# RetNet into gMLP on one core: k transposed in head pairs by 128x128 matmuls, q from the seventh block on by DMA

## The chip, the cores and the metric

One core of one Trainium2 chip. The metric is device time in microseconds; the kernel before took 252.29 us, the median of 3 runs (251.16 to 252.97).

## The reference

Retention over 8 batches, 8 heads, 576 positions, head size 64; its output, all heads side by side (512 wide), is the input of a gated MLP block that mixes along the sequence:

```python
scores = q @ k.T / sqrt(64)
ret = (scores * gamma[h] ** (i - j) * (i >= j)) @ v     # B,H,S,64
x = ret.transpose(0, 2, 1, 3).reshape(B, S, 512)
u, v = split(gelu(x @ w_in), 2)                         # 512 -> 2 x 512
v_n = (v - mean(v)) / sqrt(var(v) + 1e-6) * g_ln
v_s = w_sg @ v_n + b_sg                                 # w_sg: 576 x 576, over positions
out = x + (u * v_s) @ w_out
```

q, k, v, the weights and the output are float32; the kernel's matmuls are bfloat16.

## The kernel before

The 8 x 576 rows are cut into 18 blocks (j) of 256 rows, each of two chunks (c) of 128. The decay goes into q and v as a factor by row (the casts), so a block needs only scores, a causal mask and a state carried from chunk to chunk. A chunk's 128 rows lie on 64 partitions as (p, a), two rows side by side; c picks the half of the partitions. Stages of a block, with their lines:

- `load` (L93): k, q and v from DRAM, three transfers of 512 KB on SP's queue (more where a block crosses a batch). The pool `ld` holds three blocks.
- `cast` (L231, L238, L241): to bfloat16 with the decay factor, on POOL from block 1 on.
- `T` (L260): k and q transposed on PE, 64 matmuls of 64x64 (half of the partitions by one head), into two PSUM tiles x0 and x1, one for each chunk. ACT copies chunk 0's (L263), DVE chunk 1's (L264), each with k and q together.
- `Sc` (L279): scores, half of the heads at a time; DVE multiplies with the mask (L284, `ret`).
- `Z` (L308): the state, k times v, in PSUM (`zp`); ACT copies it (L319, `zb`).
- `inter` and `intra` (L346): the output `ot` in PSUM tag z, from the state and q, then from `ret` and v. ACT copies it to `xT` (L367), with the heads on partitions and columns as w_in's rows are.
- `V` (L374): x times the v half of w_in, into PSUM tag z; ACT takes the gelu (L377, `vg`). `moments`, `power`, `center`, `norm` make the normalized v (DVE, POOL, ACT).
- `U` (L432): the u half, into x0 and x1; ACT's gelu makes `uT`.
- `W` (L445): the mix along the sequence, a finished batch's 8 pieces spread over later blocks by `mix`; DVE multiplies with u (L449, `gT`).
- `O` (L457, L460): w_out, and x added by four matmuls with the identity, into x0 and x1; ACT copies (L462), SP stores 512 KB.

Heads: `hd(r, kk)` is 4r + kk, where r is the half of the partitions on which a head's transposed k and q lie and kk its column. A head's output goes to half h % 2, column h // 2 of `ot`, so that 128-row chunk c of w_in is its rows 128c to 128c + 127.

The order is written by hand (`manual_schedule`): each engine and each DMA queue runs in the order of the code, and waits by semaphores where data or buffers aren't ready. SP's transfers use eight semaphores in turn, so each also waits for the one eight before it. The head (L503 to L577) does blocks 0 to 2, casts the weights, and builds the transposed w_sg. In `load_head` SP's queue has block 0, the v half of w_in (`load_w("v")`), block 1, the u half, block 2; ACT's queue has the bias rows and 32 partitions of block 2. DVE casts the v half (L509) before V(0), POOL the u half (L519) before U(0). The loop (j from 3) does in turn: load j+3; half of the scores of j+1; intra(j); O; W; V(j); W; T(j+2); state matmuls and the other half of the scores of j+1; W; U(j).

Of the kernel before, what the change touches and what calls it, by code (L numbers as in the profile page):

```python
# [12 lines left out]
BF = mybir.dt.bfloat16  # L13
# [20 lines left out]
def kernel(  # L34
# [12 lines left out]
    nc = tc.nc  # L47
# [3 lines left out]
    KK = H // 2  # L51
    NT = 2 * S // 128
    NCH = B * S // 128
    NB = NCH // 2
# [19 lines left out]
    def ps2(name, shape, tag, dt=F32):  # L74
        return psD.tile(shape, dt, name=name, tag=tag)

    loaded = {}

    def load(j, eng=None, piece=None):
# [7 lines left out]
        for dst, src in ((qk[:, 1], k), (qk[:, 0], q), (vf, v)):  # L87
# [29 lines left out]

    def load_w(part):
        src = {"v": moe_w_in[:, F2:], "u": moe_w_in[:, :F2], "sg": moe_w_sg[:128 * KK], "out": moe_w_out}[part]
        nc.sync.dma_start(stage[part], src.rearrange("(c p) f -> p c f", p=128))  # L120
        if part == "sg":
            nc.sync.dma_start(wst5[:], moe_w_sg[128 * KK:])

# [93 lines left out]
    blk = {}  # L217
# [25 lines left out]
    def half(x):  # L243
        return slice(64 * x, 64 * x + 64)

    def hd(r, kk):
        return KK * r + kk

    def T(j):
        s = blk[j]  # L250
        tp = [ps2("tp", [128, 2, 2, KK, 64], f"x{c}", BF) for c in range(2)]
        rows = [[], []]
        for n, part in enumerate("kq"):
            for a in range(2):
                for kk in range(KK):
                    for c in range(2):
                        for r in range(2):
                            rows[c].append((r, 64, lambda o=tp[c][half(r), n, a, kk, :],
                                            i=s[part + "b"][half(c), a, hd(r, kk), :], c=c:
                                            nc.tensor.transpose(o, i, ident[half(c), half(c)])))  # L260
        interleave(rows)
        s["T"] = [w2.tile([128, 2, 2, KK, 64], BF, name=f"qkT{c}") for c in range(2)]
        nc.scalar.copy(s["T"][0][:], tp[0][:])  # L263
        nc.vector.tensor_copy(s["T"][1][:], tp[1][:])  # L264

    def Sc(j, g, tag="y"):
        s = blk[j]
        qkT = s["T"]
        if g == 0:
            s["ret"] = w2.tile([128, 2, KK, 2, 128], BF, name="ret")  # L270
        sc = ps2("sc", [128, 2, 2, 2, 128], tag)
        rows = [[], []]
        for x in range(2):
            kk = 2 * g + x
            for a in range(2):
                for r in range(2):
                    for c in range(2):
                        rows[r].append((c, 128, lambda o=sc[half(c), r, x, a, :], kk=kk, a=a, r=r, c=c:
                                        nc.tensor.matmul(o, qkT[c][half(r), 0, a, kk, :], qkT[c][half(r), 1, :, kk, :],  # L279
                                                         start=True, stop=True, skip_group_check=True)))  # L280
# [3 lines left out]
        nc.vector.tensor_tensor(  # L284
            s["ret"][:, :, 2 * g:2 * g + 2].rearrange("p r x a t -> p r x (a t)"),
            sc[:].rearrange("p r x a t -> p r x (a t)"),
            msk[:].rearrange("p a t -> p (a t)").unsqueeze(1).unsqueeze(1).to_broadcast([128, 2, 2, 256]),
            op=Alu.mult)
# [35 lines left out]
    def states(j, cross):  # L324


        s = blk[j]
        if "ot" not in s:
            s["ot"], s["begun"] = ps2("ot", [128, 2, KK, 2, 64], "z"), set()
        rows = [[], []]  # L330
        for r in range(2):
            c = 1 - r if cross else r
            m = (2 * j + c) % NT
            if m == 0:
                continue
            n = 32 if m == MID else 64
            for kk in range(KK):
                ro, ko = hd(r, kk) % 2, hd(r, kk) // 2
                rows[r].append((ro, 2 * n, lambda c=c, r=r, kk=kk, ro=ro, ko=ko, n=n:
                                attend(j, c, ro, s["ot"][half(ro), c, ko, :, :n], zbs[2 * j + c][half(r), kk, :],  # L340
                                       s["T"][c][half(r), 1, :, kk, :n])))
        return rows

    def attend(j, c, ro, o, *args):
        begun = blk[j]["begun"]
        nc.tensor.matmul(o, *args, start=((c, ro) not in begun), stop=True, skip_group_check=True)  # L346
        begun.add((c, ro))
# [4 lines left out]
    def intra(j):  # L352
        s = blk[j]
        rows = [[], []]
        for kk in (2, 3, 0, 1):
            for a in range(2):
                for r in range(2):
                    h = hd(r, kk)
                    ro, ko = h % 2, h // 2
                    for c in range(2):  # L360
                        rows[c].append((ro, 128, lambda c=c, a=a, r=r, kk=kk, h=h, ro=ro, ko=ko:
                                        attend(j, c, ro, s["ot"][half(ro), c, ko], s["vb"][half(c), a, h, :],
                                               s["ret"][half(c), r, kk, a, :])))
# [3 lines left out]
        nc.scalar.copy(xT[:, c0:c0 + 2].rearrange("p c k (t a) -> p (c k) a t", a=2),  # L367
                       ot[:].rearrange("p c k a t -> p (c k) a t"))
# [82 lines left out]
    def O(j):  # L451
        c0 = (2 * j) % (2 * RING)
        ob = w2.tile([128, 2, DM], F32, name="ob", tag="ob")
        for t in range(2):
            op = ps2("op", [128, DM], f"x{t}")
            for c in range(KK):
                nc.tensor.matmul(op[:], gTs[0][:, c, 128 * (c0 + t):128 * (c0 + t) + 128], w_out[:, c, :],  # L457
                                 start=(c == 0), stop=False, skip_group_check=True)
            for kk in range(KK):
                nc.tensor.matmul(op[:, 128 * kk:128 * kk + 128], xT[:, c0 + t, kk, :], ident[:],  # L460
                                 start=False, stop=True, skip_group_check=True)
            nc.scalar.copy(ob[:, t], op[:])  # L462
        nc.sync.dma_start(outf[256 * j:256 * j + 256, :].rearrange("(t p) d -> p t d", t=2), ob[:])
# [24 lines left out]
                os.append((2 * KK * (b + 1), odone[0]))  # L488
                odone[0] += 1

    HEAD = 3
    V_IN, U_IN = slice(F2, 2 * F2), slice(0, F2)

    def scores(j):
# [9 lines left out]
    fill_spares()  # L504
    cast(0, "q", nc.vector)
    cast(0, "v", nc.gpsimd)
    T(0)
    scores(0)
    nc.vector.tensor_copy(w_in[:, :, V_IN], stage["v"])  # L509
    load_w("sg")  # L510
# [3 lines left out]
    V(0)  # L514
    build_g()
    cast(1, "v", nc.gpsimd)
    T(1)
    scores(1)
    nc.gpsimd.tensor_copy(w_in[:, :, U_IN], stage["u"])  # L519
    load_w("out")  # L520
# [11 lines left out]
    split3(0, S)  # L532
    norm(0)
    load(4)
    T(2)
    moments(1, 0)
    scores(2)
    moments(1, 1)
# [17 lines left out]
    for n in range(2 * SB):  # L556
        build_wT(n)
    norm(2)
    T(3)
    Sc(3, 0)  # L560
    Z(3, 0)
    release(2)
# [2 lines left out]
    cast(4, "q", nc.gpsimd)  # L565
    cast(4, "v", nc.gpsimd)
    mix()
    T(4)
    Z(3, 1)
    inter(3)  # L570
    Sc(3, 1)
# [6 lines left out]

    for j in range(HEAD, NB):
        nx, nn = j + 1 < NB, j + 2 < NB  # L580
        if j > HEAD and j + 3 < NB:
            load(j + 3)
        if nx:
            Sc(j + 1, 0)
            Z(j + 1, 0)
        intra(j)
        if j > HEAD:
            moments(j - 1, 1)
            power(j - 1)
# [62 lines left out]
```

## Time and profile before

| what | value |
|---|---|
| runs | 251.16, 252.97, 252.29 us; median 252.29 |
| profiled execution | 254.49 us |
| its span (first to last instruction) | 252.7 us |
| mean granted TensorE clock | 0.952 |
| PE busy | 209.3 us (83%) |
| DVE, ACT, POOL busy | 159.7, 143.9, 112.1 us |
| moved by DMA | 42.82 MB, mean 169 GB/s |

How to read the rows that follow. A row of the timeline is start, duration (us), engine, line, operation, output<-input, shapes, count, and in brackets how long the engine was idle before it and what released it. The chain of work that ended last is followed back from the end, and its rows are start, duration, engine and line; "issue" there is time in which the engine waited for nothing that the profile shows. In the slices (40 equal parts of the span) a digit is the busy share in tenths. A row of windows has, for each engine, busy time and instructions, then the granted clock, the mean busy share of the 16 DMA engines, and GB/s. Queue rows give packets, MB and the share of 16 engines' time; rows of DMA issues give count, KB each and us from issue to landing. PE is the matmuls, PEld their weight loads.

### The profile page before, as it was taken

To read this page: it belongs to the slowest core of one execution; us is meant where nothing else is said; L and a number is where in the kernel's file an instruction comes from. 1 tells how busy PE (TensorE), PEld (TensorE's weight loads), DVE (VectorE), ACT (ScalarE), POOL (GpSimd) and SP (SyncE) were. 2 spreads that over 40 slices of the span, in tenths; PEclk is the share of its full clock that TensorE was granted. 3 is DMA by queue.
4 is the path that set the end of the run, shared out by engine and by line. 5 is a ranking of instruction groups with operands and counts; after the bars stand their busy time and mean duration, and the time that the engine had idled before them with its cause. 6 is when DMAs were issued, how large, how long until landed. Compare 5 with 4: busy or idle time off the path is not lost.

```text
span 252.7 us, 9232 instructions
## 1 busy us (share of the span) xinstructions
PE 209.3 (83%) x4142; PEld 145.1 (57%) x4163; DVE 159.7 (63%) x274; ACT 143.9 (57%) x211; POOL 112.1 (44%) x88
## 2 busy tenths in 40 slices
PE   0466667776799899879999979979999999999992
PEld 0433445455566666746677655647677675666551
DVE  7683987495647768857686682557595766745300
ACT  3524253675257786585675655667766758554152
POOL 6325741679923583580835638062828101101000
PEclk9998587995899999999999997999999999999999
DMA  6999999999900979980659890969382012021234
GB/s 185 313 291 247 273 308 214 206 258 182 244 6 4 289 203 281 249 153 5 195 141 237 175 258 6 237 134 284 122 230 88 21 67 86 3 83 58 110 138 194
DMA packets 63592, 42.82 MB, mean 169 GB/s; under 512 B 1529, under 2 KB 56825, under 8 KB 63554
## 3 DMA queue, kind: packets, MB, share of 16 engines
q1 hardware_dynamic: 62720, 41.83, 66.0%
q8 instruction: 32, 0.52, 1.0%
q10 hardware_dynamic: 834, 0.41, 0.8%
q14 instruction: 6, 0.05, 0.1%
HBM read 32.80 MB, written 9.44 MB: 167 GB/s over the span
## 4 chain that ended last, share of the span: by engine, by line
PE 75%; ACT 9%; DVE 8%; issue 5%; DMA 2%; ACTq 0%
PE wp L445 16%; PE hu L432 13%; PE op L457 13%; PE hv L374 12%; PE ot L346 6%; PE sc L279 5%; PE tp L260 4%; PE op L460 3%; DVE ret L284 3%; PE zp L308 3%; ACT qkT L263 2%; DMA rows<-in_moe_g_ln_dram 2%; ACT vg L377 2%; ACT xT L367 1%; DVE gT L449 1%
## 5 line engine op out<-in xcount | busy, mean ns | idle before, releaser
L395 POOL TENSOR_TENSOR rs<-rs,mhalf 128x2 f32<-128x2 f32 x18 | 19.0, 1058 | 101.9 <-DVE rs L390 78.9
L449 DVE TENSOR_TENSOR gT<-wp,uT 128x288 bf16<-128x288 f32 (+1 forms) x48 | 26.6, 555 | 44.1 <-PE wp L445 44.1
L284 DVE TENSOR_TENSOR ret<-sc,mask 128x1024 bf16<-128x1024 f32 x36 | 44.0, 1223 | 16.3 <-PE sc L279 16.1
L445 PE MATMUL wp<-wT,vn 128*128 128x288 bf16 x256 | 39.8, 289 | 1.8 <-DVE ret L284 1.3
L374 PE MATMUL hv<-w_in,xT 128*128 128x512 bf16 x138 | 35.4, 393 | 4.1 <-ACT xT L367 3.5
L432 PE MATMUL hu<-xT,w_in 128*128 128x256 bf16 x288 | 37.5, 287 | 0.8 <-ACT qkT L263 0.7
L457 PE MATMUL op<-w_out,gT 128*128 128x512 bf16 x129 | 37.4, 391 | 0.7
L241 POOL TENSOR_TENSOR vb<-vf,gv 128x1024 bf16<-128x1024 f32 x18 | 35.0, 1943 | 4.1 <-DMA vf<-in_v_dram 4.1
L434 ACT ACTIVATE uT<-hu 128x512 bf16<-128x512 f32 x36 | 21.4, 597 | 25.6 <-PE hu L432 25.6
L231 POOL TENSOR_TENSOR qb<-qk,gq 128x1024 bf16<-128x1024 f32 x17 | 34.2, 2014 | 3.3 <-DMA qk<-in_q_dram 3.3
L432 PEld LDWEIGHTS <-w_in 128*128 128x128 bf16 x288 | 29.5, 103 | 6.6 <-issue 1.1
L462 ACT COPY ob<-op 128x512 f32<-128x512 f32 x36 | 21.1, 588 | 18.1 <-PE op L460 13.0
L445 PEld LDWEIGHTS <-vn 128*128 128x128 bf16 x256 | 24.3, 98 | 11.9 <-issue 3.8
L367 ACT CAST xT<-ot 128x1024 bf16<-128x1024 f32 x18 | 23.6, 1310 | 10.9 <-PE ot L346 10.6
L377 ACT ACTIVATE vg<-hv 128x1024 f32<-128x1024 f32 x18 | 18.4, 1022 | 19.0 <-PE hv L374 19.0
L386 DVE BATCH_NORM_STATS2 bst<-vg 128x6 f32<-128x512 f32 x36 | 24.5, 682 | 3.4 <-ACT vg L377 3.4
L407 DVE SCALAR_TENSOR_TENSOR vc<-vg,mv,g_bc 128x512 f32<-128x512 f32 x36 | 25.3, 746 | 0.0
L374 PEld LDWEIGHTS <-xT 128*128 128x128 bf16 x144 | 14.1, 101 | 18.9 <-ACT xT L367 4.4
L279 PE MATMUL sc<-qkT 64*64 64x128 bf16 x576 | 16.9, 232 | 7.6 <-ACT qkT L263 6.4
L422 ACT ACTIVATE vn<-vc,rs 128x512 bf16<-128x512 f32 x32 | 21.6, 716 | 2.4 <-POOL rs L395 2.2
L319 ACT CAST zb<-zp 128x256 bf16<-128x256 f32 x32 | 12.0, 376 | 17.8 <-PE zp L308 8.9
L263 ACT COPY qkT<-tp 128x1024 bf16<-128x1024 bf16 x18 | 18.2, 1010 | 4.5 <-PE tp L260 3.9
(73 smaller groups left out, 273.5 us busy)
## 6 DMA issues: line engine op xcount, KB each, us to landing
out_dram<-ob SPq DMA_DIRECT2D x18, 512.0 KB, 2.8
qk<-in_k_dram SPq DMA_DIRECT2D x12, 512.0 KB, 6.1
qk<-in_q_dram SPq DMA_DIRECT2D x12, 512.0 KB, 7.3
vf<-in_v_dram SPq DMA_DIRECT2D x12, 512.0 KB, 8.1
wst<-in_moe_w_in_dram SPq DMA_DIRECT2D x2, 1024.0 KB, 11.0
qk<-in_k_dram SPq DMA_DIRECT2D x4, 384.0 KB, 8.4
qk<-in_q_dram SPq DMA_DIRECT2D x4, 384.0 KB, 8.1
vf<-in_v_dram SPq DMA_DIRECT2D x4, 384.0 KB, 7.9
```

What stands on the lines that cost most here:

```text
L231: eng.tensor_tensor(s["qb"][:].rearrange("p a h d -> p h a d"), qk[:, 0], bc(gq, j), op=Alu.mult)
L241: eng.tensor_tensor(s["vb"][:].rearrange("p a h d -> p h a d"), vf[:], bc(gv, j), op=Alu.mult)
L279: nc.tensor.matmul(o, qkT[c][half(r), 0, a, kk, :], qkT[c][half(r), 1, :, kk, :], start=True, stop=True, skip_group_check=True)))
L284: nc.vector.tensor_tensor(s["ret"][:, :, 2 * g:2 * g + 2].rearrange("p r x a t -> p r x (a t)"), sc[:].rearrange("p r x a t -> p r x (a t) ...
L367: nc.scalar.copy(xT[:, c0:c0 + 2].rearrange("p c k (t a) -> p (c k) a t", a=2), ot[:].rearrange("p c k a t -> p (c k) a t"))
L374: nc.tensor.matmul(hv[:, t], xT[:, (2 * j + t) % (2 * RING), kk, :], w_in[:, kk, F2:], start=(kk == 0), stop=(kk == KK - 1))
L386: nc.vector.bn_stats(bst[:], vg[:, t])
L407: nc.vector.scalar_tensor_tensor(vc[:, t], vg[:, t], mv[:, t, 0:1], g_bc[:], op0=Alu.subtract, op1=Alu.mult)
L432: nc.tensor.matmul(hu[:, i, :], w_in[:, kk, 128 * c:128 * c + 128], xT[:, c0:c0 + 2, kk, :], start=(kk == 0), stop=(kk == KK - 1), skip_gr ...
L445: nc.tensor.matmul(ps[:, i, :HS], vns[t0 + j][e][:, 128 * c:128 * c + 128], wT[:, e, j, x * HS:(x + 1) * HS], start=(j == 0), stop=(j == S ...
L449: nc.vector.tensor_tensor(o, ps[:, :, :HS], u, op=Alu.mult)
L457: nc.tensor.matmul(op[:], gTs[0][:, c, 128 * (c0 + t):128 * (c0 + t) + 128], w_out[:, c, :], start=(c == 0), stop=False, skip_group_check= ...
```

## The change

- **Heads.** `hd(r, kk)` becomes 2kk + r, so that heads 2kk and 2kk + 1 are one 128-wide column group of the natural layout. A head's output goes to half h // 4, column h % 4 (`at`). The features then lie in another order, so w_in's rows are loaded to match: each half by four transfers (n = 0 to 3), each of 2 x 64 rows of DRAM onto 128 partitions. O's identity matmuls write to permuted columns, `Sc` takes heads kk = g and g + 2, and `intra` follows. The same number of matmuls of the same shapes remains there.
- **T.** k's transposes become 8 matmuls of 128x128 (both chunks and a pair of heads at once) into tag x0, copied by DVE. q's are the same into x1, copied by ACT, for blocks 0 to 5 only.
- **q by DMA.** From block 6 on (`QDMA`), `Tdma` gives q's transposes of a block to SP as one DMA, 128 x 1024 bfloat16 from SBUF to SBUF. In the loop it stands at the start of iteration j for block j+2, between the loads of k and of q and v of block j+3. The pool for `qT` has two buffers, so it waits for the last matmul that reads qT of block j, which is in intra(j).
- **Place of T.** In the loop T(j+2) moves from behind V(j) and W to ahead of V(j).

```diff
     def load_w(part):
...
-        nc.sync.dma_start(stage[part], src.rearrange("(c p) f -> p c f", p=128))
+        if part in "uv":
+            for n in range(KK):
+                nc.sync.dma_start(stage[part][:, n], src.rearrange("(r k d) f -> k r d f", r=2, k=KK)[n])
+        else:
+            nc.sync.dma_start(stage[part], src.rearrange("(c p) f -> p c f", p=128))
...
     def hd(r, kk):
-        return KK * r + kk
+        return 2 * kk + r
+    def at(h):
+        return h // KK, h % KK
...
-    def T(j):
+    def T(j, part):
         s = blk[j]
-        tp = [ps2("tp", [128, 2, 2, KK, 64], f"x{c}", BF) for c in range(2)]
...
-                            rows[c].append((r, 64, lambda o=tp[c][half(r), n, a, kk, :],
-                                            i=s[part + "b"][half(c), a, hd(r, kk), :], c=c:
-                                            nc.tensor.transpose(o, i, ident[half(c), half(c)])))
-        interleave(rows)
-        s["T"] = [w2.tile([128, 2, 2, KK, 64], BF, name=f"qkT{c}") for c in range(2)]
-        nc.scalar.copy(s["T"][0][:], tp[0][:])
-        nc.vector.tensor_copy(s["T"][1][:], tp[1][:])
+        tp = ps2("tp", [128, 2, KK, 128], "x0" if part == "k" else "x1", BF)
+        for a in range(2):
+            for kk in range(KK):
+                nc.tensor.transpose(tp[:, a, kk, :], s[part + "b"][:, a, 2 * kk:2 * kk + 2].rearrange("p h d -> p (h d)"), ident[:])
+        s[part + "T"] = w2.tile([128, 2, KK, 128], BF, name=part + "T")
+        if part == "k":
+            nc.vector.tensor_copy(s["kT"][:], tp[:])
+        else:
+            nc.scalar.copy(s["qT"][:], tp[:])
+
+    def Tdma(j):
+        s = blk[j]
+        s["qT"] = w2.tile([128, 2, KK, 128], BF, name="qT")
+        nc.sync.dma_start_transpose(s["qT"][:].rearrange("p a k t -> p (a k) t"),
+                                    s["qb"][:].rearrange("p a h d -> p (a h d)"))
...
-                nc.tensor.matmul(op[:, 128 * kk:128 * kk + 128], xT[:, c0 + t, kk, :], ident[:],
+                nc.tensor.matmul(op[:].rearrange("p (r k d) -> p k r d", r=2, k=KK)[:, kk], xT[:, c0 + t, kk, :], ident[:],
                                  start=False, stop=True, skip_group_check=True)
...
-    HEAD = 3
+    HEAD, QDMA = 3, 6
...
     for j in range(HEAD, NB):
         nx, nn = j + 1 < NB, j + 2 < NB
         if j > HEAD and j + 3 < NB:
-            load(j + 3)
+            load(j + 3, parts="k")
+        if nn and j + 2 >= QDMA:
+            Tdma(j + 2)
+        if j > HEAD and j + 3 < NB:
+            load(j + 3, parts="qv")
...
             release(j - 1)
+        if nn:
+            T(j + 2, "k")
+            if j + 2 < QDMA:
+                T(j + 2, "q")
         V(j)
         mix()
-        if nn:
-            T(j + 2)
```

SP's queue at the start of the program (names are output<-input, `wst` is the stage of the weights, sizes are of the SBUF side; a wait names one of the eight DMA semaphores). Before:

```order
L93 DMA vf<-in_v_dram 128x8x128
L120 DMA wst<-in_moe_w_in_dram 128x4x512
L93 DMA qk<-in_k_dram 128x8x128 [waits DMAHW0_49]
L93 DMA qk<-in_q_dram 128x8x128 [waits DMAHW2_49]
L93 DMA vf<-in_v_dram 128x8x128 [waits DMAHW4_49]
L120 DMA wst<-in_moe_w_in_dram 128x4x512 [waits DMAHW5_49]
```

And now, in the same place:

```order
L94 DMA vf<-in_v_dram 128x8x128
L123 DMA wst<-in_moe_w_in_dram 128x1x512 x2
L123 DMA wst<-in_moe_w_in_dram 128x1x512 [waits DMAHW0_49]
L123 DMA wst<-in_moe_w_in_dram 128x1x512 [waits DMAHW1_49]
L94 DMA qk<-in_k_dram 128x8x128 [waits DMAHW3_49]
L94 DMA qk<-in_q_dram 128x8x128 [waits DMAHW5_49]
L94 DMA vf<-in_v_dram 128x8x128 [waits DMAHW7_49]
L123 DMA wst<-in_moe_w_in_dram 128x1x512 [waits DMAHW0_49]
L123 DMA wst<-in_moe_w_in_dram 128x1x512 [waits DMAHW1_49]
L123 DMA wst<-in_moe_w_in_dram 128x1x512 [waits DMAHW2_49]
L123 DMA wst<-in_moe_w_in_dram 128x1x512 [waits DMAHW3_49]
```

Each half of w_in is four transfers where it was one; their place among the loads of blocks 0 and 1 is the same.

SP's queue in the loop, from one store of the output to the next. Before:

```order
L463 DMA out_dram<-ob 128x2x512 [waits DMAHW5_49,Activation_49]
L93 DMA qk<-in_k_dram 128x8x128 [waits DMAHW6_49,Pool_49]
L93 DMA qk<-in_q_dram 128x8x128 [waits DMAHW7_49]
L93 DMA vf<-in_v_dram 128x8x128 [waits DMAHW0_49,Pool_49]
L463 DMA out_dram<-ob 128x2x512 [waits DMAHW1_49,Activation_49]
```

Now (a block whose loads are cut in two by the end of a batch):

```order
L94 DMA qk<-in_k_dram 96x8x128 [waits DMAHW0_49]
L94 DMA qk<-in_k_dram 32x8x128 [waits DMAHW1_49]
L275 DMA_TRANSPOSE qT<-qb 128x8x128 [waits DMAHW2_49,PE_49,Pool_49]
L94 DMA qk<-in_q_dram 96x8x128 [waits DMAHW3_49]
L94 DMA qk<-in_q_dram 32x8x128 [waits DMAHW4_49]
L94 DMA vf<-in_v_dram 96x8x128 [waits DMAHW5_49]
L94 DMA vf<-in_v_dram 32x8x128 [waits DMAHW6_49]
L475 DMA out_dram<-ob 128x2x512 [waits DMAHW7_49,Activation_49]
```

The transpose waits for PE and POOL, and the loads of q and v and the store stand behind it on the queue.

PE in the loop, the end of T and what follows it. Before (64 pairs of a weight load and a matmul, k's then q's, with Z behind them):

```order
L260 LDWEIGHTS qb
L260 MATMUL tp<-ident,qb 64x64
L308 LDWEIGHTS kb
L308 MATMUL zp<-vb,kb 64x64
L308 LDWEIGHTS kb
```

Now (8 pairs, k's alone, with V behind them):

```order
L265 LDWEIGHTS kb
L265 MATMUL tp<-ident,kb 128x128
L386 LDWEIGHTS xT
L386 MATMUL hv<-w_in,xT 128x512
L386 LDWEIGHTS xT
```

T stands ahead of V and has 16 rows where it had 128; Z follows the W that follows V. PE's whole program has 6408 rows where it had 8328.

More of the change, by code (lines that the diff above doesn't have):

```diff
@@ L77, with load @@
     loaded = {}
-    def load(j, eng=None, piece=None):
+    def load(j, eng=None, piece=None, parts="kqv"):
         if j not in loaded:
@@ L86, in load @@
         spans = sorted(zip(cuts[:-1], cuts[1:]), key=lambda s: s[0] - s[1])
-        for dst, src in ((qk[:, 1], k), (qk[:, 0], q), (vf, v)):
+        for part in parts:
+            dst, src = {"k": (qk[:, 1], k), "q": (qk[:, 0], q), "v": (vf, v)}[part]
             for n, (lo, hi) in enumerate(spans):
@@ L246, in hd @@
     def hd(r, kk):
-        return KK * r + kk
-    def T(j):
+        return 2 * kk + r
+    def at(h):
+        return h // KK, h % KK
+    def T(j, part):
         s = blk[j]
-        tp = [ps2("tp", [128, 2, 2, KK, 64], f"x{c}", BF) for c in range(2)]
[L252 to L257, printed above, removed]
-                            rows[c].append((r, 64, lambda o=tp[c][half(r), n, a, kk, :],
-                                            i=s[part + "b"][half(c), a, hd(r, kk), :], c=c:
-                                            nc.tensor.transpose(o, i, ident[half(c), half(c)])))
-        interleave(rows)
-        s["T"] = [w2.tile([128, 2, 2, KK, 64], BF, name=f"qkT{c}") for c in range(2)]
-        nc.scalar.copy(s["T"][0][:], tp[0][:])
-        nc.vector.tensor_copy(s["T"][1][:], tp[1][:])
+        tp = ps2("tp", [128, 2, KK, 128], "x0" if part == "k" else "x1", BF)
[12 more added lines that the diff above has]
+                                    s["qb"][:].rearrange("p a h d -> p (a h d)"))
     def Sc(j, g, tag="y"):
         s = blk[j]
-        qkT = s["T"]
         if g == 0:
@@ L273, in Sc @@
         for x in range(2):
-            kk = 2 * g + x
+            kk = g + 2 * x
             for a in range(2):
@@ L278, in Sc @@
                         rows[r].append((c, 128, lambda o=sc[half(c), r, x, a, :], kk=kk, a=a, r=r, c=c:
-                                        nc.tensor.matmul(o, qkT[c][half(r), 0, a, kk, :], qkT[c][half(r), 1, :, kk, :],
+                                        nc.tensor.matmul(o, s["kT"][half(r), a, kk, half(c)], s["qT"][half(r), :, kk, half(c)],
                                                          start=True, stop=True, skip_group_check=True)))
@@ L284, in Sc @@
         nc.vector.tensor_tensor(
-            s["ret"][:, :, 2 * g:2 * g + 2].rearrange("p r x a t -> p r x (a t)"),
+            s["ret"][:, :, g::2].rearrange("p r x a t -> p r x (a t)"),
             sc[:].rearrange("p r x a t -> p r x (a t)"),
@@ L336, in states @@
             n = 32 if m == MID else 64
-            for kk in range(KK):
-                ro, ko = hd(r, kk) % 2, hd(r, kk) // 2
+            for kk in (0, 2, 1, 3):
+                ro, ko = at(hd(r, kk))
                 rows[r].append((ro, 2 * n, lambda c=c, r=r, kk=kk, ro=ro, ko=ko, n=n:
                                 attend(j, c, ro, s["ot"][half(ro), c, ko, :, :n], zbs[2 * j + c][half(r), kk, :],
-                                       s["T"][c][half(r), 1, :, kk, :n])))
+                                       s["qT"][half(r), :, kk, 64 * c:64 * c + n])))
         return rows
@@ L354, in intra @@
         rows = [[], []]
-        for kk in (2, 3, 0, 1):
+        for g in (1, 0):
             for a in range(2):
                 for r in range(2):
[L358 to L363, printed above, removed]
+                    for kk in (g, g + 2):
+                        h = hd(r, kk)
+                        ro, ko = at(h)
+                        for c in range(2):
+                            rows[c].append((ro, 128, lambda c=c, a=a, r=r, kk=kk, h=h, ro=ro, ko=ko:
+                                            attend(j, c, ro, s["ot"][half(ro), c, ko], s["vb"][half(c), a, h, :],
+                                                   s["ret"][half(c), r, kk, a, :])))
         interleave([x + y for x, y in zip(rows, states(j, False))])
@@ L506 @@
     cast(0, "v", nc.gpsimd)
-    T(0)
+    T(0, "k")
+    T(0, "q")
     scores(0)
@@ L516 @@
     cast(1, "v", nc.gpsimd)
-    T(1)
+    T(1, "k")
+    T(1, "q")
     scores(1)
@@ L534 @@
     load(4)
-    T(2)
+    T(2, "k")
+    T(2, "q")
     moments(1, 0)
@@ L558 @@
     norm(2)
-    T(3)
+    T(3, "k")
+    T(3, "q")
     Sc(3, 0)
@@ L567 @@
     mix()
-    T(4)
+    T(4, "k")
+    T(4, "q")
     Z(3, 1)
```

## The prediction

> **What bounds the kernel now.** I read the page first (busy time, slices, chain), then the chain of work in order of time for one block of the loop, then the timeline of the first 35 us, then the DMA views of that stretch.
>
> ```profile
> span 252.7 us, 9232 instructions
> PE 209.3 (83%) x4142; PEld 145.1 (57%) x4163; DVE 159.7 (63%) x274; ACT 143.9 (57%) x211; POOL 112.1 (44%) x88
> DMA  6999999999900979980659890969382012021234
> PE 75%; ACT 9%; DVE 8%; issue 5%; DMA 2%; ACTq 0%
> ```
>
> Three quarters of the chain that ended last is PE. DMA is only 2% of it, but the slices show the 16 DMA engines full from about 6 to 63 us, so whatever adds work to a DMA engine there has no free time to hide in. The loop is PE behind PE; here is one block of it in the chain:
>
> ```profile
> 186.47 0.59 PE ot L346 x39
> ...
> 190.57 1.73 PE hv L374 x8
> 192.29 0.61 PE wp L445 x5
> 192.91 0.64 PE tp L260 x64
> 193.54 0.37 PE zp L308 x16
> ...
> 196.84 0.35 PE sc L279 x16
> ...
> 197.43 0.59 PE ot L346 x34
> ```
>
> From one intra to the next it is 10.96 us, all of it PE. A microsecond more before the loop is therefore a microsecond more at the end: the loop has no idle PE to take it back. The head waits otherwise. These rows of the timeline are the ones that matter:
>
> ```profile
> 8.97 1.93 POOL L241 TENSOR_TENSOR vb<-vf,gv 128x1024 bf16<-128x1024 f32 x1 [4.07 <-DMA vf<-in_v_dram]
> ...
> 14.19 1.22 DVE L509 CAST w_in<-wst 128x2048 bf16<-128x2048 f32 x1
> ...
> 25.13 1.89 POOL L519 CAST w_in<-wst 128x2048 bf16<-128x2048 f32 x1 [2.67 <-DMA wst<-in_moe_w_in_dram]
> ...
> 29.84 3.60 PE L432 MATMUL hu<-xT,w_in 128*128 128x256 bf16 x16
> ```
>
> The first loads have landed at 8.97 us, the V half of w_in is cast at 14.19, the U half has just landed at 25.13, and U(0), its first user, starts at 29.84.
>
> **The change, part by part.**
>
> *The w_in rows.* Each half was one transfer of 1 MB, 128 rows against 128 rows. Now it is four, whose DRAM side has 2 as its outer count (heads r) and whose SBUF side has 128. How many DMA engines such a transfer gets decides this case. The nearest rows are the ACT queue's:
>
> ```profile
> q10 hardware_dynamic: 834, 0.41, 0.8%
> ...
> qk<-in_k_dram ACTq DMA_DIRECT2D x1, 128.0 KB, 7.3
> ...
> rows<-in_moe_b_sg_dram ACTq DMA_DIRECT2D x2, 6.8 KB
> rows<-in_moe_g_ln_dram ACTq DMA_DIRECT2D x1, 6.0 KB
> ```
>
> That queue carried three loads of 32 x 8 rows (768 packets of 512 B) and three of 3 rows (9 packets): 777. The other 57 of its 834 packets hold no data. If every engine that takes part ends a transfer with one packet, 57 = 3 x 16 + 3 x 3: sixteen engines for an outer count of 32, three for an outer count of 3. So the outer count limits the engines. What no row shows is which side counts when the sides differ, 2 against 128. I take the smaller, two engines, since an engine that takes whole outer steps finds only two of them in the source; the other end is sixteen, at no cost. I also take the same two for all eight; were they spread by turns, the four of a half would run side by side and the cost would be near that of sixteen. The Trainium skill, "DMA: Bandwidth & Descriptors" (section on why a DMA increments its semaphore by 16), says that the engine count is the largest number up to 16 that divides the slowest dimension of both sides, and that the lowest-numbered engines are taken. By it all eight transfers run on the same two engines and the sum is the one below; by the SBUF side alone it would be rival B's.
>
> What two engines move, from windows in which the 2 KB rows of w_in pass, and one with 512 B rows (GB/s is the last column, for sixteen engines):
>
> ```profile
> 7.00:8.00 1.00, 0.63 (x32) 0.50 (x32) 0.96 (x4) 0.06 (x1) 0.00 (x0) 1.00 1.17 304
> ...
> 9.00:10.00 1.00, 0.24 (x20) 0.10 (x8) 0.69 (x1) 0.99 (x3) 1.00 (x1) 1.00 1.06 386
> ...
> 19.00:20.00 1.00, 1.00 (x4) 0.30 (x2) 0.00 (x0) 0.00 (x0) 1.00 (x1) 1.00 1.05 381
> ...
> 32.00:33.00 1.00, 1.00 (x6) 0.71 (x5) 0.97 (x2) 0.36 (x1) 1.00 (x2) 0.50 1.05 353
> ```
>
> 381 / 16 = 23.8 GB/s for one engine, 47.6 for two: 1.049 MB take 22.0 us. The two engines also carry their sixteenth of everything else, in the order of the queue: block 0 until 8.97; the ACT queue's piece of block 2, 0.39 MB at 304 GB/s, 1.3 us; the V half, 22.0; block 1's 1.57 MB, 5.2; the U half, 22.0. 8.97 + 1.3 + 22.0 + 5.2 + 22.0 = 59.5 us. Then POOL's cast, 1.89, and U(0) starts at 61.4 instead of 29.84: **+31.5**. Everything ahead of U(0), V(0) from 32.5 us and block 1 with it, fits into this wait, the ACT queue too, whose third load now waits for the first w_in piece. After U(0) the order is the old one; k and q of block 2 stand right behind on the queue (3 x 1.3 us) and POOL takes them in its old order. DVE has done its bias splitting in the wait, but T(2) did not wait for that before. At 353 GB/s a half takes 23.8 (+35); at 430, which some slices of 0.05 us between 19 and 21 us reach, 19.5 (+26.5):
>
> ```profile
> GB/s 430 307 430 379 389 389 348 389 297 471 389 389 338 379 369 410 369 451 287 410 410 369 410 328 451 369 410 369 328 420 266 379 451 236 369 358 317 338 328 389
> ```
>
> *T on PE.* Before, 64 matmuls of 64x64 a block, 0.64 us in the chain. Now eight of 128x128 for k, and eight for q in blocks 0 to 5. The same shape stands in O:
>
> ```profile
> 119.13 0.22 PE op L460 x4
> ```
>
> So eight take 0.44. From block 6 on that is 0.20 less by the chain, but some 0.1 of the 0.64 is the change from 128-wide work to 64x64, which now falls to Z: 12 x -0.1 = -1.2. Blocks 2 to 5 take 0.88 for 0.64: +1.0; blocks 0 and 1 hide in the wait. Sum 0; ends -2.4 and +1.5.
>
> *Copies and covers.* ACT loses the copy of q (1.01 us) in twelve blocks. In the chain it stands at one place of the last rows:
>
> ```profile
> 159.82 0.91 ACT vg L377
> 160.73 0.01 issue
> 160.74 1.01 ACT qkT L263
> ```
>
> And the wait for xT in a block without an O:
>
> ```profile
> 109.23 1.90 PE L374 MATMUL hv<-w_in,xT 128*128 128x512 bf16 x7 [0.39 <-ACT xT L367]
> ```
>
> The copy's going saves about 1.0 at that place. T(k) before V fills the wait for xT in blocks without an O (three such blocks, 0.39 in the row below, together -1.0). But T no longer stands between V and the state matmuls, which need the bank that vg frees: 0.61 + 0.37 of cover is left for vg's 1.02 and its hand-over, some 0.1 late in ten blocks, and 0.7 in the two that have no W there: +2.4. Sum +0.4, ends -2 and +4.
>
> *Gaps without a releaser.* In the loop the chain has four long "issue" gaps:
>
> ```profile
> 105.98 0.77 issue
> ...
> 112.66 1.39 issue
> ...
> 150.10 1.97 issue
> ...
> 165.61 1.36 issue
> ```
>
> ```profile
> q8 instruction: 32, 0.52, 1.0%
> ```
>
> 5.5 us, inside or behind bursts of small matmuls, one right behind T. The queues' view has 32 transfers of instructions, and PE's program shrinks from 8328 rows to 6408. If PE runs out of instructions there, fewer rows mean fewer gaps. The cause isn't shown, so I take half, -2.9; ends 0 and -7 (with the slower matmuls after 150.10).
>
> *The DMA transposes.* One of 256 KB a block on SP, from block 6. It waits for POOL's q (done a block before) and for the last matmul of intra(j), which reads the buffer that it overwrites; behind it wait q and v of block j+3 and the output. Its reader is Sc(j+2, 0): intra ends at 187.06, Sc starts at 196.84, so 9.8 us are free. No row shows a transposing DMA. The nearest:
>
> ```profile
> out_dram<-ob SPq DMA_DIRECT2D x18, 512.0 KB, 2.8
> ...
> DMA to landing us min/median/max: 4.3/7.4/13.2
> ...
> 177.99 1.06 POOL L395 TENSOR_TENSOR rs<-rs,mhalf 128x2 f32<-128x2 f32 x1 [5.58 <-DVE rs L390]
> ```
>
> Low end 2.8 (output, an idle queue, twice the bytes), high end 13.2 (the slowest load of k or q). With the queue nearly idle at that time I take the low end: hidden, 0. The q and v loads go out some 6 us later than now, and POOL's casts of them start up to 2 us later; its 5.58 us of idle time a block covers that.
>
> **Sum.** +31.5 + 0 + 0.4 - 2.9 + 0 = +29. The profiled execution took 254.5 us (span 252.7, 1.8 around it), 0.9% over the median of 252.3; I put the difference on the median: 252.3 + 29 = **281 us**.
>
> **The rivals.**
> - *B, the copies use all sixteen engines all the same* (the SBUF side's 128 decides, or the pairs change by turns). Then the w_in term is 0 and what is left is -2.5: 249.8, from 245 to 254, not slower. For it: all that a queue needs, 1 MB in 128 rows, is unchanged. Against it: the 3-row copies.
> - *C, the transposes land late.* It decides from 9.8 us after intra(j). At 13.2 Sc would wait 3.4 in each of twelve blocks: 281 + 41 = 322; one just over the bound costs a few us. Against it: the output's 2.8. The Trainium skill, "VectorE: DVE Perf Modes" (section on the three transpose paths), gives 1309 ns for a 128x128 bf16 transpose by DMA; eight in a row would be an estimated 10.5 us, 0.7 late in each block, and the sum 289. No run here shows it, and the DMA page named above gives 261 GB/s, 1 us for 256 KB, which is no cost.
> - *D, the wait is real but work after it runs together*: the loop starts with loads and casts further ahead; up to 5 us come back, 276. The head's waits behind U(0) are on ACT and DVE by their own work, which speaks against it; it is inside my range.
>
> **How the numbers follow.** Forecast with D 0.84, B 0.10, C 0.06. The forecast's own ends: fast engines and all gaps gone, 281 - 5 - 4 - 4 = 268; slow engines, no gap gone, covers at their worst, 281 + 3.5 + 3 + 5 = 293. That leaves out B, nearly all of C and little else, under 2 in 10, so the range is 268 to 293. A change of 1% (2.5 us) is about what a measurement of this kernel can tell from none. Slower: 0.84 + 0.06 = 0.90; B lies at the lower edge of "within 1%", so it gives 0.05 faster and 0.05 same.
>
> **What would show it.** Right: the POOL cast of the U half waits for wst until 55 to 64 us and U(0) starts behind it; V(0) waits until about 32; the mean DMA share between 10 and 58 us falls far below 0.9 while two engines work; the loop's block stays near 10.9 us; no wait for qT by Sc. Wrong: U(0) near 30 us (B); Sc or its weight load waiting for a DMA of qT (C); more or longer "issue" gaps than 5.5 us in the loop (that term); T(k) of 0.6 us or more; a wait of ot for vg well over 0.1 a block.

## The result, and the profile after

The changed kernel took 284.53 us, the median of 4 runs (283.62 to 285.16); the kernel before took 252.63 us beside it (4 runs, 251.16 to 253.22). The ratio is 1.127, 95% interval 1.121 to 1.133: slower by 31.9 us. The profiled execution of the changed kernel took 283.62 us, with a span of 281.8 us and a mean granted clock of 0.974. Against the profiled execution of the kernel before the span grew by 29.1 us; the rest of the 31.9 is that before's profiled execution (254.49 us) is one of its slow ones, 1.9 us over the median, and this one lies 0.9 us under its own.

The page of the changed kernel: the span, the busy times, the DMA slices, the shares of the chain of waits.

```profile
span 281.8 us, 7308 instructions
...
PE 210.8 (75%) x3182; PEld 148.1 (53%) x3203; DVE 157.8 (56%) x274; ACT 133.1 (47%) x199; POOL 112.8 (40%) x88
...
DMA  7314511559999920899987986979996730220334
...
q8 instruction: 25, 0.41, 0.6%
...
PE 57%; SPq 13%; ACT 10%; DMA 9%; DVE 6%; issue 2%; POOL 1%; ACTq 0%; POOLq 0%; DVEq 0%
```

PE has as much work as before (210.8 us, 209.3 before), but its share fell from 83% to 75%: the new time is idle time. The DMA slices show where: before they stood at 9 from the second slice on, now the second to the eighth (7 to 56 us) read 3, 1, 4, 5, 1, 1, 5. SP's queue and DMA, 2% of the chain before, are 22% now. The timeline of the head:

```profile
32.36 1.23 DVE L522 CAST w_in<-wst 128x2048 bf16<-128x2048 f32 x1 [10.59 <-DMA wst<-in_moe_w_in_dram]
...
60.62 1.89 POOL L533 CAST w_in<-wst 128x2048 bf16<-128x2048 f32 x1 [20.50 <-DMA wst<-in_moe_w_in_dram]
...
62.56 3.60 PE L444 MATMUL hu<-xT,w_in 128*128 128x256 bf16 x16 [15.46 <-POOL w_in L533]
```

The V half's cast stands at 32.36 us (14.19 before), the U half's at 60.62 (25.13), and U(0) starts at 62.56 (29.84), released by that cast after 15.46 us of idle PE. Windows of the two stretches in which the halves pass (the last two columns are the mean share of the 16 DMA engines and GB/s):

```profile
10.00:32.00 22.00, 3.83 (x104) 3.21 (x103) 2.45 (x2) 4.42 (x6) 0.93 (x1) 1.00 0.32 94
...
36.00:58.00 22.00, 7.55 (x133) 5.19 (x130) 10.97 (x15) 4.66 (x6) 4.12 (x2) 1.00 0.27 80
```

80 GB/s with a quarter of the engines' time, where the head of before moved 381 at a share of 1.05. Both windows also hold loads of k, q and v, which raise these figures. Here are two shorter ones, in which w_in is alone under way:

```profile
12.00:14.00 2.00, 0.00 (x0) 0.00 (x0) 0.00 (x0) 0.00 (x0) 0.00 (x0) 1.00 0.13 46
...
30.00:32.00 2.00, 0.00 (x0) 0.00 (x0) 0.00 (x0) 0.00 (x0) 0.00 (x0) 1.00 0.13 48
```

A share of 0.13 is 2.1 of the 16 engines, so two are at work. All four transfers of the V half had been issued by 16.9 us, and the share was still 0.13 from 30 to 32 us, so they are the same two for all four. The head thus became 32.7 us longer. The rest of the program gave some of it back:

| profiled execution | U(0) starts | U(0) to U(3) | U(3) to end | span |
|---|---|---|---|---|
| before | 29.8 | 45.5 | 177.4 | 252.7 |
| after | 62.6 | 46.8 | 172.5 | 281.8 |

Of the 4.9 us that the part behind U(3) lost, the twelve blocks that follow give 5.6 and the end takes 0.7 back. Three of them, those with before's "issue" gaps, went from 11.76, 14.17 and 11.42 us to 10.12, 10.27 and 10.13, together 6.8 us less; the other nine are 1.2 longer, all together. (Behind U(3) the blocks of the changed kernel, e1 and e5 agree with each other to 0.01 us: what happens in the head only shifts the loop.) One block of the loop in the chain now:

```profile
176.40 0.45 PE tp L265 x8
176.84 1.74 PE hv L386 x8
178.59 0.02 issue
178.61 1.03 ACT vg L389
179.64 0.04 issue
179.68 0.30 PE ot L357 x6
179.99 0.22 PE sc L290 x16
180.21 0.72 PE wp L457 x5
180.93 1.75 PE hu L444 x16
182.67 0.35 PE sc L290 x16
```

T takes 0.45 us (0.64 before), and a new step stands behind V: ACT's gelu `vg`, 1.03 us, for which the next matmuls into tag z wait. Only then come `ot`, the scores and U.

### The profile page after: what moved, and what is told of

Its sections match the earlier page's. It is cut to its first block, busy times and chain, and to the rows that moved or that the text cites. A ratio compares the mean times of both kernels' runs of the same rounds, so it can differ in the third digit from the quotient of the medians.

```text
span 281.8 us, 7308 instructions
## 1 busy us (share of the span) xinstructions
PE 210.8 (75%) x3182; PEld 148.1 (53%) x3203; DVE 157.8 (56%) x274; ACT 133.1 (47%) x199; POOL 112.8 (40%) x88
## 4 chain that ended last, share of the span: by engine, by line
PE 57%; SPq 13%; ACT 10%; DMA 9%; DVE 6%; issue 2%; POOL 1%; ACTq 0%; POOLq 0%; DVEq 0%
PE hu L444 12%; PE wp L457 12%; PE op L469 9%; PE hv L386 9%; DMA wst<-in_moe_w_in_dram 8%; SPq L123 7%; SPq L94 6%; ACT vg L389 5%; PE ot L357 4%; PE sc L290 4%; PE tp L265 3%; PE op L472 2%; DVE ret L295 2%; DMA out_dram<-ob 1%; PE zp L319 1%
## 5 line engine op out<-in xcount | busy, mean ns | idle before, releaser
L469 PE MATMUL op<-w_out,gT 128*128 128x512 bf16 x129 | 36.1, 380 | 1.3 <-ACT ob L474 0.5
L389 ACT ACTIVATE vg<-hv 128x1024 f32<-128x1024 f32 x18 | 18.4, 1022 | 29.8 <-PE hv L386 29.7
L474 ACT COPY ob<-op 128x512 f32<-128x512 f32 x36 | 21.0, 588 | 16.0 <-PE op L472 10.9
L243 POOL CAST kb<-qk 128x1024 bf16<-128x1024 f32 x17 | 18.4, 1080 | 24.8 <-DMA qk<-in_k_dram 24.8
L290 PE MATMUL sc<-qT,kT 64*64 64x128 bf16 x576 | 16.8, 234 | 13.8 <-ACT qT L270 12.8
L268 DVE COPY kT<-tp 128x1024 bf16<-128x1024 bf16 x18 | 12.3, 684 | 20.0 <-PE tp L265 20.0
```

The source lines that it names most:

```text
L290: nc.tensor.matmul(o, s["kT"][half(r), a, kk, half(c)], s["qT"][half(r), :, kk, half(c)], start=True, stop=True, skip_group_check=True)))
L389: nc.scalar.activation(vg[:], hv[:], Act.Gelu_apprx_tanh)
```

## The experiments

The theory: the w_in transfers run on two DMA engines because their DRAM side has an outer count of 2, and that is the whole loss. Its rivals: that each transfer more costs time by itself; that 128 rows on the SBUF side decide; that the transposes on SP add to it. From e5 on the smaller terms were tried: the place of T, and the gaps.

**e1: w_in with an outer count of 64.** The changed kernel, with each of the four transfers of a half cut in two, so that each takes 64 rows of DRAM to 64 partitions.

```diff
-                nc.sync.dma_start(stage[part][:, n], src.rearrange("(r k d) f -> k r d f", r=2, k=KK)[n])
+                for r in range(2):
+                    nc.sync.dma_start(stage[part][64 * r:64 * r + 64, n],
+                                      src.rearrange("(r k d) f -> k r d f", r=2, k=KK)[n, r])
```

> The changed kernel, with each half of w_in loaded by eight transfers of 64 rows (outer count 64 on both sides) instead of four of 2 x 64. Two-engine theory: the outer count of 2 is the whole cost; with 64 on both sides all sixteen engines take part, POOL's cast of the u half starts near 25 to 28 us, U(0) near 30, and what is left is the loop's gain, 219.2 us from U(0) to the end where it was 222.9: 249 us (246 to 252). Rival, transfer count: the four transfers a half and the eight semaphores in turn hold SP's queue up; eight transfers a half are then no better, 280 us or more. Rival, the loop: the DMA transposes and the lost cover cost something that the wait in the head hides; then 253 us or more.

Measured: 254.42 us (252.73 to 256.05), ratio to before 1.0139 (1.0085 to 1.0193). With twice the transfers 30 us are gone, so the count of transfers isn't the cause. It is still 5.4 us over the forecast of 249, and over its range, where the rival of a slower loop (253 or more) lies. But the loop isn't the cause: from U(0) to the end e1's profiled execution took 218.5 us, and 219.2 were counted on. The head has 3.7 of the 5.4: U(0) starts at 33.7 us and not near 30. Another 2.0 us lie around the span, which the forecast left out. The timeline of e1's head:

```profile
11.62 1.28 ACT L517 ACT_TABLE_LOAD   x1 [4.70 <-DMA wst<-in_moe_w_in_dram]
13.02 0.99 ACT L272 COPY qT<-tp 128x1024 bf16<-128x1024 bf16 x1
...
16.72 1.23 DVE L297 TENSOR_TENSOR ret<-sc,mask 128x1024 bf16<-128x1024 f32 x1 [0.74 <-PE sc L292]
17.87 1.37 DVE L524 CAST w_in<-wst 128x2048 bf16<-128x2048 f32 x1
```

ACT issues three loads of block 2 itself, and stood still for 4.70 us until a transfer of w_in had landed. So its copy of q's transposes came at 13.02 us (9.65 in e5; ACT's copy of T stood at 9.34 before), the scores and DVE's product with the mask followed, and the V half's cast, which stands right behind that product in DVE's order, came at 17.87 (14.19). Each is 3.7 us later than before, and between product and cast DVE wasn't idle: the cast was late by ACT's wait.

**e2 and e3: the kernel before, with only the w_in transfers of the change, outer count 2, then 4.** Everything else is before's.

```diff
-        nc.sync.dma_start(stage[part], src.rearrange("(c p) f -> p c f", p=128))
+            for n in range(KK):
+                nc.sync.dma_start(stage[part][:, n], src.rearrange("(r k d) f -> k r d f", r=2, k=KK)[n])
```

(e3 has r=4 in place of r=2.)

> The kernel before, with w_in alone loaded as in the changed kernel (four transfers of 2 x 64 rows a half), the rest left; w_in's rows then lie in another order than x's columns, so the product is another one of the same size. Two-engine theory: the U half's cast starts near 60 us and the time is 252.6 + 32 = 285 us (281 to 289). If the wait needed the rest of the change as well, less: 253 to 270.

> As e2_before_outer_2, with 4 x 32 rows instead of 2 x 64 in each of the four transfers a half (w_in's rows again in another order than x's columns). Two-engine theory, four engines here: a half takes 11 us, so the U half lands near 8.97 + 1.3 + 11 + 5.2 + 11 = 37.5 us, U(0) starts near 40.4 and the time is 252.6 + 10.5 = 263 us (260 to 267). Rival, transfer count: the count is the same as with 2 x 64, so the time is the same, 285 us. Rival, spread by the SBUF side: 252.6.

Measured, two runs each: e2 286.0 us (285.5 to 286.51), ratio 1.1398 (1.1307 to 1.1488); e3 266.92 (266.44 to 267.4), ratio 1.0637 (1.0553 to 1.0722). e3 lies at the upper edge of its range: its U half was cast at 40.8 us, where 37.5 was forecast for the landing. The two casts of w_in in e2, then in e3 (mean ns, then their start):

```profile
L513 DVE CAST w_in<-wst x1: 1227/1227/1227, 32.5 to 32.5; 128x2048 bf16<-128x2048 f32 x1
L523 POOL CAST w_in<-wst x1: 1890/1890/1890, 60.2 to 60.2; 128x2048 bf16<-128x2048 f32 x1
```

```profile
L513 DVE CAST w_in<-wst x1: 1226/1226/1226, 22.6 to 22.6; 128x2048 bf16<-128x2048 f32 x1
L523 POOL CAST w_in<-wst x1: 1889/1889/1889, 40.8 to 40.8; 128x2048 bf16<-128x2048 f32 x1
```

The w_in transfers alone make the whole loss: e2's casts stand within 0.5 us of the changed kernel's. From one cast to the next are 27.7 us with an outer count of 2 and 18.2 with 4. With the SBUF side deciding, both distances would be as before (10.9). The number of transfers is the same in e2 and e3, so it isn't what sets them apart. The engines at work are seen in e3's windows too, where w_in is alone:

```profile
10.00:12.00 2.00, 0.00 (x0) 0.00 (x0) 0.00 (x1) 0.00 (x0) 1.17 (x1) 1.00 0.26 96
```

0.26 of 16 are 4.2 engines, with 96 GB/s, where two had 46 to 48.

**e4: e1, with all of q's transposes on PE.**

```diff
-    HEAD, QDMA = 3, 6
+    HEAD, QDMA = 3, NB
```

> As e1_w_in_sixteen, with q transposed by PE in all blocks (no DMA transposes): 12 x 8 more matmuls of 128x128 on PE and 12 more copies of 1.01 us on ACT. If the loop is bound by PE and the DMA transposes are hidden: 12 x 0.44 = 5.3 us slower than e1_w_in_sixteen, less some 0.1 a block that the longer T gives back as nothing waits there: 253 to 255 where e1 is 249. Rival, the loop's gain comes from fewer rows of PE (fewer gaps): within 2 us of e1. Rival, the transposes cost time in the loop: e4 is as fast as e1 or faster.

Measured: 259.82 us (258.75 to 261.38), 5.4 us over e1; ratio to before 1.0365 (1.0307 to 1.0423). 5.3 was forecast (12 x 0.44), but that they meet is luck: in the profiled executions the twelve blocks from U(3) on are 7.3 us longer than e1's, 0.6 each and not 0.44, while U(0) stands 2.1 us earlier (31.6, 33.7 in e1). So q's transposes cost more on PE than PE's own time for them, and by DMA they are hidden.

**e5: w_in by two transfers a half.** The changed kernel; each transfer has 64 as its outer count on both sides.

```diff
-            for n in range(KK):
-                nc.sync.dma_start(stage[part][:, n], src.rearrange("(r k d) f -> k r d f", r=2, k=KK)[n])
+            for r in range(2):
+                nc.sync.dma_start(stage[part][64 * r:64 * r + 64],
+                                  src.rearrange("(r k d) f -> r d k f", r=2, k=KK)[r])
```

> The changed kernel with each half of w_in in two transfers of 64 rows x 4 columns (outer count 64 on both sides), where e1_w_in_sixteen had eight. In e1 U(0) started at 33.7 us (29.8 before), since the V half was cast at 17.9 (14.2) and ACT's queue waited behind the many transfers. If that is the whole of it, the V half is cast near 14.5, U(0) starts near 30 to 31, and the time is e1's 254.4 - 3 = 251.5 us (249.5 to 253), level with the kernel before. Rival: U(0) is late by the 128x128 transposes of blocks 0 and 1 and their two copies; then 254 as in e1.

Measured: 250.93 us (12 runs, 249.66 to 252.34), ratio 0.9985 (0.9947 to 1.0023): the change without its w_in cost can't be told from the kernel before. Its casts, and a stretch of its head as a window:

```profile
L523 DVE CAST w_in<-wst x1: 1218/1218/1218, 15.1 to 15.1; 128x2048 bf16<-128x2048 f32 x1
L534 POOL CAST w_in<-wst x1: 1889/1889/1889, 27.7 to 27.7; 128x2048 bf16<-128x2048 f32 x1
```

```profile
10.00:20.00 10.00, 5.71 (x109) 3.69 (x109) 6.52 (x7) 2.71 (x4) 3.33 (x3) 1.00 1.15 255
```

The DMA engines are full again (1.15), and U(0) starts at 29.6 us. The head isn't quite as before: the U half is cast 2.6 us later (25.13 there), and U(0) to U(3) is 2.4 us longer.

**e6: e5, with T(j+2) behind V(j) and the mix, its old place.**

```diff
+        V(j)
+        mix()
         if nn:
             T(j + 2, "k")
...
-        V(j)
-        mix()
```

> As e5_two_a_half, with T(j+2) behind V(j) and its W, as in the kernel before. In the changed kernel's chain vg (1.03 us) stands ahead of the state matmuls in nearly every block, and a block takes 0.1 to 0.2 us more than before. If the lost cover is the cause, T's 0.45 us covers it again: a block back at 10.7, 1.5 us less than e5. Rival: T ahead of V pays for it by covering xT; then within 0.5 of e5, or slower by about 1.

Measured: 248.73 us (247.68 to 249.15), 2.2 less than e5, where 1.5 was forecast; ratio 0.9887 (0.9841 to 0.9933), so 1.1% faster than before. The wait of `ot` for vg, as "its engine sat idle before it" has it for the output tile (us in all, times), in before, in the changed kernel and in e6:

```profile
  ACT vg L377: 1.4, 4
```

```profile
  ACT vg L389: 4.6, 8
```

```profile
  ACT vg L390: 3.3, 6
```

(e5, like the changed kernel, has 4.6 in 8.) From e5 to e6, of the twelve blocks that follow U(3), seven fell by 0.32 to 0.45 us and one by 0.18, two stayed, and two grew by 0.42 and 0.32: together 2.2 us less, which is what the medians show. The wait for vg gives 1.3 of them (4.6 to 3.3); what the rest is stays open. One that grew is where T no longer fills the wait for xT (9.79 to 10.21), the other has an "issue" gap of 0.35.

**e7: the kernel before, with 64 more small matmuls ahead of T(0).** They are transposes of the identity that nobody reads; they move everything behind them in PE's program by 64 weight loads and change nothing else.

```diff
+    dm = ps2("dm", [128, 16, 64], "w", BF)
+    for n in range(64):
+        nc.tensor.transpose(dm[:64, n % 16, :], ident[:64, :64], ident[:64, :64])
```

> The kernel before with 128 rows more at the start of PE's program (64 transposes of the identity that nobody reads, while PE waits for k). The five gaps of PE's weight loads of over 1 us in the profile of before that had no releaser stand at row 190 + 256 n of its weight loads and matmuls. If PE waits there for the next 256 instructions, the gaps keep to 190 + 256 n with the new rows counted, so they leave their old places (the zp matmuls ahead of intra(11), the O that follows intra(12)) for others, and their sum changes by chance: time 249 to 254. Rival, the places themselves (a buffer, a clock, a semaphore): the same gaps at the same instructions.

Measured: 259.18 us (4 runs, 257.41 to 261.12), ratio 1.031 (1.0228 to 1.0391). Where the gaps lie: windows from the start to each gap of over 1 us that the chain has in the kernel before (27.97 is ahead of U(0)). The second count in brackets is PEld's, the weight loads up to there:

```profile
0.00:27.97 27.97, 12.80 (x350) 8.85 (x351) 18.70 (x43) 10.43 (x15) 13.77 (x22) 0.92 1.04 256
...
0.00:112.66 112.66, 82.32 (x1879) 57.91 (x1887) 78.62 (x135) 61.24 (x89) 65.61 (x56) 0.91 0.93 219
0.00:150.10 150.10, 118.19 (x2644) 83.43 (x2655) 104.69 (x179) 85.55 (x124) 84.45 (x68) 0.93 0.87 205
0.00:165.61 165.61, 131.03 (x2898) 91.61 (x2911) 112.99 (x191) 93.94 (x136) 90.30 (x72) 0.93 0.85 198
```

And in e7:

```profile
0.00:85.16 85.16, 62.62 (x1375) 44.71 (x1375) 58.67 (x102) 42.68 (x62) 49.78 (x44) 0.88 0.95 218
0.00:97.43 97.43, 73.02 (x1631) 51.98 (x1631) 66.08 (x114) 49.96 (x73) 55.63 (x48) 0.89 0.92 216
0.00:130.12 130.12, 102.74 (x2271) 72.49 (x2271) 88.89 (x153) 70.72 (x103) 73.18 (x60) 0.91 0.87 205
0.00:143.83 143.83, 114.94 (x2527) 80.68 (x2527) 97.66 (x167) 78.46 (x115) 79.03 (x64) 0.92 0.86 199
0.00:188.14 188.14, 155.37 (x3423) 108.87 (x3423) 126.16 (x215) 108.10 (x157) 102.43 (x80) 0.94 0.84 199
```

351, 1887, 2655 and 2911, and 1375, 1631, 2271, 2527 and 3423: each is 95 plus a multiple of 128 (256, 1792, 2560, 2816; 1280, 1536, 2176, 2432, 3328). A weight load and its matmul are two rows, so the gaps come at steps of 256 rows of PE's program, and the program's 6408 rows in the changed kernel by its 25 transfers of instructions are 256.3 (before, 8328 by 32, 260). The times of those transfers say the same: ahead of each of the nine gaps one of 16 KB begins, 0.7 to 1.5 us earlier, and the gap ends 1.3 to 1.7 us after it has ended (for the gap of 112.66 to 114.05 us, 111.18 to 112.53). So PE waits there for its own instructions, as far as the traces can tell. The shift didn't move the steps; it moved the code under them, and other bursts of small matmuls were hit. The size was forecast wrongly: the loop's gaps of over 0.5 us in the chain grew from 5.5 to 8.8 us, and U(3) to the end from 177.4 to 182.2. What the other 1.5 of these 4.8 us are, and what the median has beyond them, stays open.

**e8: e6, with q by DMA from block 5 on** (QDMA 5 in place of 6).

> As e6_T_behind_V, with q by DMA from block 5 on instead of 6. One block less of q on PE (0.44 us) and on ACT (1.01 us): 0.5 us less than e6 (0 to 1). Rival: block 5's transpose stands on SP's queue ahead of loads that are late there (the DMA engines are still full), and costs 1 us or more.

Measured: 248.47 us (247.61 to 249.19), ratio to before 0.9885 (0.9834 to 0.9935). It is 0.3 less than e6, where 0.5 was forecast (0 to 1), and these runs can't tell it from none. e6 and e8 are the best versions: 1.1% faster than before.

## Why the prediction was right, point by point

The direction, the cause and the size held: 281 us was forecast, from 268 to 293, and 284.53 measured. The terms of its sum:

*w_in, +31.5.* Measured +32.7 at U(0): the U half was cast at 60.6 us (59.5 forecast) and U(0) started at 62.56 (61.4). e2 shows that the transfers do this alone, e3 that four engines for an outer count of 4 cost half as much transfer time, e5 that it all but goes away with an outer count of 64 on both sides. That the smaller side counts and that the engines are the same two for all transfers were the forecast's assumptions, and the share of 0.13 with all four transfers issued bears both out: with two engines of its own for each, it would have been higher. At 48 GB/s a half of 1.049 MB takes 21.8 us (22.0 in the forecast). The Trainium skill, "DMA: Bandwidth & Descriptors" (section on why a DMA increments its semaphore by 16), has the engine count as a divisor of the slowest dimension of both sides: e2, e3 and e5 agree, with 286.0, 266.92 and 250.93 us for 2, 4 and 64. Rival B, sixteen engines, fell with U(0). It had for it that bytes and rows were unchanged, which is true and didn't matter.

*T on PE, 0.* Eight 128x128 took 0.45 us by the chain, 0.44 forecast. U(0) to U(3), where q is on PE as well, is 1.3 us longer (+1.0 was forecast for the blocks with q on PE). That the two are close proves little: with the same PE code there, it is 0.9 longer in e1 and 2.4 in e5. What T alone saves in the later blocks (-1.2 forecast) was not measured by itself.

*Copies and covers, +0.4.* The lost cover of vg was forecast at +2.4; the wait grew by 3.2, from 1.4 to 4.6, and e6 got 2.2 us back by putting T where it was. The step was right, and the wait a third larger. e6 still has 3.3 where before had 1.4; T covers 0.45 us there now instead of 0.64, which fits but was not tried by itself. ACT's copy of q (1.01) stood in before in the block of 14.17 us, together with the gap of 1.97; that block fell by 3.9, which has room for the -1.0.

*Gaps without a releaser, -2.9.* This is the term that was mis-sized. All of them went: the loop's chain of the changed kernel has no "issue" of over 0.3 us, so the term is -5.5, inside its ends (0 and -7). The gaps of 5.5 and the copy of 1.0 make 6.5 of the 6.8 us by which the three blocks fell. The gaps are no accident of that one execution: e3, with the same loop, has 130.31 us from U(3) to U(15) where before has 130.34, and gaps of over 1 us in the same three blocks. e7 gives the cause that the forecast left open. Why none of them comes in the changed kernel wasn't isolated: T is 16 rows now and not 128, so a burst ends sooner and there are fewer steps (25 transfers, not 32). All kernels with 128-wide transposes (after, e1, e4, e5, e6, e8) have no "issue" of over 0.9 us in the chain, and none over 0.72 behind U(3), while before, e2, e3 and e7, with the 64-wide ones, have three to five of over 1 us in the loop.

*The DMA transposes, 0.* The low end of the landing was taken, 2.8 us. The tile qT in the changed kernel:

```profile
L275 SPq DMA_TRANSPOSE qT<-qb x12: 1232/1236/2434, 112.6 to 226.2; - x12
...
DMA to landing us min/median/max: 3.5/3.6/3.7
```

3.6 us, against 9.8 that are free: rival C is far off. SP's queue waits for them a good deal, as this list of waits has it, and no one on the path waits for it:

```profile
SPq L275 <- PE ot L357: 71.9, 12, 17.5
...
SPq L275 <- POOL vb L246: 3.9, 7, 1.0
```

No matmul waits for a DMA of qT, and e4 shows the price without them, 5.4 us. The Trainium skill, "VectorE: DVE Perf Modes" (section on the three transpose paths), would have given an estimated 10.5 us for these eight 128x128 pieces; the runs have 3.6 and decide.

*The sum.* +29 was forecast, against before's profiled execution, and its span did grow by 29.1: +32.7 for w_in, +1.3 for the head's blocks, -4.9 behind them. That the sum fits so well is luck in part: w_in and the head's blocks came out 2.5 us dearer than forecast, and the loop won 2.4 us more. The 3.5 us by which 281 missed are mostly the step that "put the difference on the median": the +29 holds between two single executions, of which before's was 1.9 us over its median and the changed kernel's 0.9 under. e5 has the same difference: what is left of the change without w_in was forecast at -2.5; between the profiled spans it is -2.8 (249.9, 252.7), between the medians -0.6 us (ratio 0.9985). What makes before's profiled execution longer than its median isn't shown.

*Rival D*, up to 5 us of the wait coming back, isn't seen: U(0) to U(3) grew.

Open: which of the smaller loop terms (T, the wait for xT) gives how much by itself, and the end, 0.7 us longer; out's stores land after a median of 5.9 us instead of 2.8, over the whole run.

## What to carry to other kernels

When a rearrangement of heads is paid for by loading weights in another row order, look at the outer count of each transfer's both sides: the weights by an outer count of 2 cost 33.6 us (284.53 against e5's 250.93), and another way of writing the same load, by 64 rows, gave that back. Cutting a load into many transfers can cost by itself, through an engine that issues loads of its own and must wait behind them: e1's sixteen began U(0) 4.0 us later than e5's four. A change with one large cost can hide a small gain: it was found only when the cost was removed and the moved step was put back. A moved step loses the wait that it covered where it was, so count what it leaves uncovered, and not only what it covers.

## What the runs showed of the hardware beyond that

PE stopped for 1.2 to 2.0 us at steps of 256 rows of its program where small matmuls run fast, each time within 1.5 us of the start of a transfer of instructions. The same code with 64 unread matmuls ahead of it was 3.1% slower (ratio 1.0228 to 1.0391), so a difference of a per cent or two between kernels of many small matmuls may be the place of the code and not its merit. e6's 1.1% is of that size: its loop won 7.9 us from U(3) to U(15) (130.34 to 122.47), and 5.5 of them are before's gaps. Here is the gap of before behind T, in the timeline:

```profile
112.36 0.30 PE L346 MATMUL ot<-qkT,zb 64*64 64x128 bf16 x7
114.05 0.24 PE L346 MATMUL ot<-qkT,zb 64*64 64x128 bf16 x1 [1.39 <-issue]
```

It cuts a group of eight like matmuls in two, after the seventh: no data, no buffer and no other engine is between them.
